# Turning a kernel's token weights on TensorE in float32, with the cast in the eviction, under a new order of all steps

## The chip, the cores and the metric

The kernel runs on one core of a Trainium2 chip. The metric is the device time of one execution in microseconds (us). The engines are TensorE (PE in the profile; its weight loads are listed as PEld), VectorE (DVE), ScalarE (ACT), GpSimd (POOL) and SyncE (SP), which here issues every DMA. TensorE writes to PSUM, eight banks of 128 partitions by 512 float32; VectorE and ScalarE read PSUM, GpSimd doesn't.

## The reference

q, k and v have 8 batches, 8 heads, 576 tokens and 64 columns. Attention has two parts that are added: one over means of four tokens, repeated four times, and one over the neighbours at a distance under 4. The result x, 8 x 576 x 512, goes through a channel-mixing block with token weights:

```
q_d, k_d, v_d = means of 4 tokens;  out_up = repeat(softmax(q_d k_d') v_d, 4)
out_local     = softmax(q k' where |i - j| < 4) v
x             = out_up + out_local, as batch x token x (head, column)
theta = x @ w_theta
zr, zi = x * cos(theta), x * sin(theta)
y = w_tok_r @ zr + w_tok_i @ zi            # 576 x 576 weights over tokens
u = x + y
out = u + max(u @ w_ch, 0)
```

## The kernel before, in words

Each batch runs through the same steps; each has a two-letter name in the code. k and q are loaded (lk, lq) into 16 float32 staging slots (st), cast to bf16 (ck, cq, L296; on VectorE a cast is two instructions, one of 512 columns and one of 64), turned on TensorE (tp, L303) and copied out of PSUM to kT and qT (ev, L316). Means of four tokens are taken on VectorE or GpSimd (kd, qd, L322 or L330 and L333/L336). v is loaded in two halves (lv, lw) and cast (cv, L396); for batch 0 it is loaded in long rows (l1), cast (c1, L372), turned and placed by TensorE (t1, e1, x1, L377 to L394). Scores and their exponentials go through PSUM (sd, ed, ps, ex), the neighbour mask is multiplied in on VectorE or GpSimd (mk, L501), products and normalisation follow (po, nm, nd, xn), and xt and xa give x transposed (xT, L541). Then come theta (th, L552), cosine and sine on ScalarE (cs), z (xm, zz), the mixing with the token weights (mx, L632: eight groups a batch, each of nine matmuls of 288 columns), u (ua, L637), its transposed copy for the residual (up and uc, or the DMA transpose du), the channel weights (ch, L662), the last sum (rl, L667) and the store (st).

The token weights are needed as WT, nine tiles of 128 x 576 bf16 with the summed token on the partitions. The two matrices together have nine row blocks: 0 to 3 are real, 5 to 8 imaginary, and block 4 has the last 64 rows of each. Before, a block is loaded (lb), cast to bf16 into the tiles uT, which serve as room for it (cb, L261), and when all nine are there, each of the nine column tiles is turned by five bf16 transposes into one bank (wp, L273; the last tile by ten) and copied to WT (wc, L278).

The order of the work is written out by hand in ORDER, a list of words: the step's name and a place, which is a staging slot, one or two PSUM banks, or the engine (v VectorE, a ScalarE, g GpSimd). Each engine, and the DMA queue on SyncE, gets its instructions in the order of the list and keeps to it, so a step that waits holds all that stands behind it on its engine. Words that begin with wm are matmuls on zeros (L755) that fill TensorE's time; ts and te load ScalarE's tables (L761). pin() makes the order binding.

Of the kernel before, what the change touches and what calls it, by code (L numbers as in the profile page):

```python
# [41 lines left out]
WPJ = (0, 2, 4, 6, 1, 3, 5, 7, 8)  # L42
# [20 lines left out]
cbg lw cbg cqg lw xa xm1 nm th6 xt23 lv6 evv th7 ts cs xa zz tp45 cbg cbg wp0 cs wcv lv3 xm6 cs tt2 xm3 th7 wp1 lw xm0
zz zz lw qdv lk8 wcv eva ct lk4 lq9 cs cbg cbg cbg cbg wp6 wca wp3 wp2 wp4 wp5 wca wp1 wcv wcv wcv wp2 ztg ps67 ps45
qdg wcv te ex wcv ex lq7 kdg lkb lka zz lkc lqe lkd zp1 zcv cvv lqf mx3 cvg cvg cvg mkv ua cvg lq1 mx2 sd01 ps67 lv0
mkv lq2 ex po45 mx3 nm sd67 ua cqg po45 ed lw po01 nm ua nm mx2 ed ua pv67 po45 lq5 mx3 cqg vda nm nd01 ua cka up2
nd67 mkg cka xn ckg ckg lk6 uca xn up3 tp45 uca tp01 xd6 eva ckg xt23 mx7 xcv eva qdg xa xt45 po01 th6 cqg xa lv3 ckg
lv9 tp23 nm ts cs cqa th4 lq7 xm5 xt01 th6 evv cs tp23 xa zz cqa tt4 ua tp01 kdg cs ct cqg evv ztv th5 lw evv lw xm7
zz cs tp23 mx6 xm4 kdg zp5 qdg ua eva zz cvv ps01 cqa ps23 lv8 xm7 kdg zz zcv lk4 te ex lw mx6 mx4 ua mx5 sd01 mkv lvb
lw ua ex po67 mkv cva ps23 qdg lca lcc utg ed lce nm mx4 cvg ex lcd lvf ua lk1 po01 lk2 sd67 lw po23 ckg nm cqa nm mx5  # L70
ckg ed tp01 cvg ua lq5 eva tp67 mx4 lq0 cca ua up5 evv cvg ua ccg ccg pv23 mkg ucv vda lk3 qdv ps01 ps67 ex up4 mx5
ccv nd23 ex ua nd01 uca kdg ch5 po67 xn ps23 ckg cka lv9 mx4 xn tp01 lw ex mkg rl nm lk6 cva ckg xd5 sd23 ua cqg xcv
xt67 lv7 eva mx4 lw lv4 lw cvg xa lv8 lw ed xt01 po23 po67 th5 ua ch4 cqa ts cs xa nm nm th0 po23 lqb xt67 rl up1 cs
nm kdg th5 xm0 xa cs xm4 tp23 xm6 tt7 mkg cvg zz th0 lqc ucv zz st up1 cvg up5 ch4 eva ucv ckg ct ucv ch1 zz po23 cs
sd67 lve lva rl mkv te ed cvg pv45 lqd lk1 ztg cqg ch0 rl rl lk2 ch1 qdg nm lq3 vda tp67 nd45 rl cqa xm0 lqf eva lw zz
xn nd23 zp1 utg lw xn tp67 zca lk5 lq9 kdg mx0 up1 ua po45 lv0 eva ckg lk7 ps23 nm lw po67 nm ckg lv4 uca mx0 tp45 lk6
qdg mx1 ua xd0 ps67 ua lv8 ex eva xca ckg sd23 xt45 xa lw mx1 mkg st cvg ua ed mx0 ex mx1 mkv ua th0 po23 ua xt45 ts
cs xa xt67 mx1 xm0 xa th4 xm5 lqb zz ua tt0 kdg xm1 cvv ckg cvv th6 ch7 cqg cka cqg cs ct nm cs lvc cqg lk1 ztv tp23
eva lw th0 rl zz cs cqg zz tp67 evv cvg xm4 zz st zp5 zca ch1 rl cva tp23 mx0 po67 ua eva ps45 lw nm po23 lv2 te ex
lv5 mx1 pv67 lke cqg st mx0 po45 dt vda nm lk7 mkv st lqd po23 ckg ua ua qdg sd67 ch1 qdg nm nm ht0 cka ed rt lv3 up6  # L80
up7 cvg ucv uca nd45 kdg cqg nd23 mx0 xn lw xn ps67 ss ps45 ex ex xd2 mx3 tp67 xcv up2 cva ua uca tp45 lq6 rl evv up0
cqg lw eva ch1 ua lvf xt67 ps23 ucv sd45 xa cva st ex lw lq9 rl lk4 mx0 sd23 ed xt67 ua ckg xa lva qdg lw mkv kdv xt45
mx1 cvg th0 ua st lvb mx6 ua lw ed mkg tp23 ts cs utg lw mx7 cqg xa ua up6 po01 po45 cvg eva uca pv23 tt7 nm vda lq0
nm th6 xm0 zz nd45 ct cs ch1 lv1 xn cva st tp23 nd67 cva xn up0 th4 xm5 th6 zz sr eva xm7 xm5 ps23 lv8 lvc rl uca cs
po01 ch4 zz lw cs nm zz ztg ch7 te ex dz xd6 ch5 cvg rl lw lqe utg rl mkg po01 ps23 st mx4 lw lkd up7 cqg cka st ex
up2 uca nm ch3 rl xt01 kdg st st cvg xcv cva qdg ckg ua xa mkg uca po45 pv67 mx2 nm mx0 ua lk6 sd45 vda lk2 rl lq7
xt67 cqg ua ps23 xa mx1 lv5 ed po45 ua lq3 nm st mkv cqg dt ex dk9 sd23 xt67 ckg ed mx0 mkg du xa nd45 ch1 ckg ua po23
xn po67 th0 ts cs th4 tt5 nm cs nd23 rl dkf nm ct cqg evg dka xm1 xm0 mx6 zz th1 th7 cs dk1 cs xm4 xm5 zz ztv xn ua zz
mx6 zz mx4 po23 ua dz xt01 po67 xd5 ua xcv eva lw evg mx4 nm st mx5 eva du xa mx2 ht3 qdg ua mx4 xt01 ua kdg nm ua utg
ps67 du rt cvv du st ps23 kdg ua te ex ex mx5 mx4 ps67 lvb lv0 lw lw qdv xa lv8 sd23 cva xt01 ua mkv xa mkg mx5 ex st  # L90
lv4 ua po67 ua ed nm sd01 ed po23 mkg cvg ch4 ch5 mx0 nm tt1 lw lw cvg cvg rl sr po67 rl dxd po23 ua nm po45 nm ts ct
nm th0 pv67 th1 dx vda ch2 ztg nd45 st st nd67 du xn du xn cs cs du th3 cs th0 xd1 xt45 xt67 rl xcv cs xt23 xa utg dxc
ch1 dx zz ch0 ch4 xa ss ch5 dz th6 zz ch7 dt du xa tt2 zz th3 dxe dx zz st cs rl th1 mx6 cs mx3 ct st ua rl ztv rl cs
dx7 dx mx2 th6 ht4 rt zz mx1 ua mx0 cs rl mx3 mx6 zz dz rl zz ua ua zz mx7 mx1 mx2 ua ua mx0 ua mx3 ua mx6 ua ua mx1
st ua du mx0 st mx2 ua ss utv ch3 ua ua ua st ua utv ch2 ch1 ch0 ch7 ch6 du ch4 du du du du st rl sr rl du du rl dt
ch1 st st rl st rl st st rl rl ht0 rl st st rm su rt sr ss st
# [4 lines left out]
def kernel(  # L101
# [91 lines left out]
    def constants():  # L193
# [3 lines left out]
        nc.vector.memset(warm, 0.0)  # L197
# [61 lines left out]
    def cb(i, w):  # L259
        to = uT[0][:, i, :] if i < 5 else uT[1][:, i - 5, :]  # L260
        COPY[w](out=to, in_=at.pop(("wtok", i)))  # L261
# [15 lines left out]
    def wc(j, w):  # L277
        COPY[w](out=WT[:, j, :], in_=at.pop(("wp", j))[:, 0:S])  # L278
# [520 lines left out]
```

## Time and profile before

| what | value |
|---|---|
| median of 3 runs | 237.85 us (236.62 to 238.53) |
| profiled execution: span from its first to its last instruction | 232.1 us |
| the median less that span | 5.75 us |
| instructions | 9462 |
| DMA | 49.41 MB, mean 213 GB/s |

The profile is of one execution; it gives the span alone, and 5.75 us is what the median of the runs has beside it. Rows are read as follows. A group has its line in the kernel, engine and operation, what it writes and what it reads (partitions x elements, type), its count, busy time, the mean time of one in ns, and the idle time of the engine ahead of it with what ended it. A row of a tile's or a line's view has the least, the median and the longest time of one in ns, and the first and the last start in us. A row of the time line has its start and length in us, and the chain of waits in order of time has the same. A row of stages has the length of the stage, the busy time and number of instructions of each engine in it, the granted share of TensorE's clock, the share of the DMA engines' time, and GB/s.

### The profile page before, as it was taken

What the parts mean: (1) busy time and instruction counts of PE and PEld (TensorE: products, weight loads), DVE (VectorE), ACT (ScalarE), POOL (GpSimd) and SP (SyncE); (2) the same over time, 40 slices, a digit from 0 to 9 for tenths busy, and PEclk for the clock granted to TensorE, in tenths of its full rate; (3) what the DMA queues carried; (4) which work ended last, traced back from release to release, by engine and by line L of the source; (5) the groups of instructions that cost most, each with busy time, mean ns of one, the idle gap of its engine ahead of it and who ended that gap; (6) DMA issues with size and microseconds to landing.
All of it is one profiled execution on the core that took longest, in us unless ns stands there. A gap on an engine that the chain in (4) does not pass through costs nothing.

```text
span 232.1 us, 9462 instructions
## 1 busy us (share of the span) xinstructions
PE 220.7 (95%) x3986; PEld 153.2 (66%) x3986; DVE 191.8 (83%) x365; ACT 156.1 (67%) x241; POOL 135.5 (58%) x179
## 2 busy tenths in 40 slices
PE   7998899999998999999999999999999998999991
PEld 2665678777776765776768766676676563767750
DVE  6699999989997988868997997799889967567572
ACT  3359999799877989867976979857766591620000
POOL 7468989869999656897472837767386510000000
PEclk9999999999999999999999999999999999999998
DMA  6999989999999899989606895899957766556676
GB/s 204 382 392 390 298 134 252 365 263 193 264 263 195 224 290 208 203 209 210 174 3 178 226 234 147 293 249 173 153 122 189 144 138 100 154 126 182 138 235 217
DMA packets 76795, 49.41 MB, mean 213 GB/s; under 512 B 61136, under 2 KB 61392, under 8 KB 76752
## 3 DMA queue, kind: packets, MB, share of 16 engines
q1 hardware_dynamic: 76752, 48.81, 84.6%
q8 instruction: 31, 0.51, 1.1%
q14 instruction: 12, 0.10, 0.2%
HBM read 33.98 MB, written 9.44 MB: 187 GB/s over the span
## 4 chain that ended last, share of the span: by engine, by line
PE 72%; DVE 12%; DMA 5%; SPq 3%; issue 3%; ACT 2%; DVEq 0%
PE PS L632 24%; PE PS L662 10%; PE PS L552 9%; PE PS L303 5%; PE PS L755 4%; PE PS L511 3%; DVE xT L541 3%; DMA out_dram<-osb 2%; DVE pm L501 2%; PE PS L591 2%; PE PS L482 2%; DMA st<-xT 2%; SPq L641 2%; PE PS L533 2%; DVE uT L637 2%
## 5 line engine op out<-in xcount | busy, mean ns | idle before, releaser
L632 PE MATMUL PS<-WT,z 128*128 128x288 bf16 x576 | 77.9, 286 | 1.7 <-issue 1.7
L632 PEld LDWEIGHTS <-z 128*128 128x128 bf16 x576 | 53.8, 98 | 17.5 <-issue 2.8
L637 DVE TENSOR_TENSOR uT<-PS,xT 128x288 bf16<-128x288 f32 x64 | 28.1, 450 | 11.4 <-PE PS L632 11.1
L552 PE MATMUL PS<-wth,xT 128*128 128x512 bf16 x128 | 32.3, 380 | 0.7 <-DVE xT L541 0.7
L557 ACT ACTIVATE cs<-PS,pihc 128x512 bf16<-128x512 f32 x32 | 22.3, 696 | 15.1 <-PE PS L552 9.9
L662 PE MATMUL PS<-wch,uT 128*128 128x512 bf16 (+1 forms) x132 | 30.6, 373 | 0.0
L520 DVE TENSOR_TENSOR tmp<-PS,rl 128x512 bf16<-128x512 f32 x40 | 27.7, 692 | 1.4
L541 DVE TENSOR_TENSOR xT<-PS,xdT 128x928 bf16<-128x928 f32 (+1 forms) x24 | 22.7, 952 | 3.4 <-PE PS L533 3.1
L490 ACT ACTIVATE pm<-PS 128x1024 bf16<-128x1024 f32 (+1 forms) x24 | 20.4, 877 | 7.0 <-PE PS L482 2.7
L501 POOL TENSOR_TENSOR pm<-pm,band 128x1024 bf16<-128x1024 bf16 (+1 forms) x13 | 22.2, 1709 | 2.9 <-ACT pm L490 2.9
L667 DVE SCALAR_TENSOR_TENSOR osb<-PS,ur 128x512 f32<-128x512 f32 (+1 forms) x33 | 21.8, 669 | 2.4 <-PE PS L662 1.6
L330 POOL TENSOR_TENSOR two<-kT 128x580 f32<-128x580 bf16 x15 | 17.5, 1163 | 6.1 <-ACT kT L316 5.2
L296 POOL CAST q_tm<-st 128x576 bf16<-128x576 f32 x22 | 14.4, 664 | 10.8 <-DMA st<-in_q_dram 10.8
L662 PEld LDWEIGHTS <-uT 128*128 128x128 bf16 x132 | 12.2, 98 | 12.2 <-issue 0.3
L558 ACT ACTIVATE cs<-PS 128x512 bf16<-128x512 f32 x32 | 19.4, 605 | 0.0
L330 POOL TENSOR_TENSOR two<-qT 128x576 f32<-128x576 bf16 x11 | 12.8, 1167 | 10.5 <-ACT qT L316 7.1
L552 PEld LDWEIGHTS <-xT 128*128 128x128 bf16 x128 | 11.2, 98 | 10.7 <-issue 1.3
L616 DVE TENSOR_TENSOR z<-PS,cs 128x1024 bf16<-128x1024 bf16 x24 | 16.2, 685 | 1.9 <-PE PS L591 0.9
L437 ACT ACTIVATE pd<-PS 128x864 bf16<-128x864 f32 x16 | 14.1, 889 | 5.2 <-PE PS L426 5.2
L761 ACT ACT_TABLE_LOAD x13 | 16.7, 1283 | 0.2
L296 POOL CAST k_tm<-st 128x576 bf16<-128x576 f32 x21 | 14.4, 695 | 1.4 <-DMA st<-in_k_dram 1.4
L396 POOL CAST v_w<-st 128x512 bf16<-128x512 f32 x21 | 13.3, 653 | 1.3 <-DMA st<-in_v_dram 1.2
(119 smaller groups left out, 419.3 us busy)
## 6 DMA issues: line engine op xcount, KB each, us to landing
st<-in_q_dram SPq DMA_DIRECT2D x32, 288.0 KB, 6.3
st<-in_k_dram SPq DMA_DIRECT2D x32, 288.0 KB, 6.0
st<-in_v_dram SPq DMA_DIRECT2D x70, 128.0 KB, 4.7
out_dram<-osb SPq DMA_DIRECT2D x31, 256.0 KB, 2.9
out_dram<-osb SPq DMA_DIRECT2D x10, 128.0 KB, 2.4
st<-in_v_dram SPq DMA_DIRECT2D x4, 288.0 KB, 3.7
st<-in_moe_w_tok_r_dram SPq DMA_DIRECT2D x4, 288.0 KB, 6.2
st<-in_moe_w_tok_i_dram SPq DMA_DIRECT2D x4, 288.0 KB, 7.2
```

The costliest lines, as they stand in the source:

```text
L296: COPY[w](out=to[:, r, :], in_=of[:, r, :])
L330: nc.gpsimd.tensor_tensor(out=t, in0=src[:, :, 0:2], in1=src[:, :, 2:4], op=ALU.add)
L490: nc.scalar.activation(out=pm[(3 * b + u) % NPM][:, :, 0:n].rearrange("p e c j w -> p e (c j w)"), in_=at.pop(("ps", b, u))[:, :, 0:4 * W ...
L501: EW[w].tensor_tensor(out=t, in0=t, in1=m, op=ALU.mult)
L520: nc.vector.tensor_tensor(out=tmp[(NCH * b + c) % NTMP].rearrange("p g (j d) -> p g j d", d=D), in0=ps[:, :, :, 0:D], in1=r.unsqueeze(3).t ...
L541: nc.vector.tensor_tensor(out=xT[b % 2][:, :, lo:lo + cnt].rearrange("p e (m j) -> p e m j", j=4), in0=at.pop(("xt", b, u))[:, :, 0:cnt].r ...
L552: nc.tensor.matmul(out=ps, lhsT=xT[b % 2][:, dc, P * c:P * c + P], rhs=wth[:, dc, :], start=(dc == 0), stop=(dc == 3))
L557: nc.scalar.activation(out=t[:, 0, :], in_=ps, func=AF.Sin, bias=pihc, scale=1.0)
L632: nc.tensor.matmul(out=ps, lhsT=z[b % 2][:, j, P * dc:P * dc + P], rhs=WT[:, j, cols], start=(j == 0), stop=(j == 8))
L637: nc.vector.tensor_tensor(out=uT[b % 2][:, dc, cols], in0=at.pop(("mx", b, i)), in1=xT[b % 2][:, dc, cols], op=ALU.add)
L662: nc.tensor.matmul(out=ps[:, cols], lhsT=uT[b % 2][:, dc, P * c:P * c + P], rhs=wch[:, dc, cols], start=(dc == 0), stop=(dc == 3))
L667: nc.vector.scalar_tensor_tensor(out=o[:, cols], in0=at["ch", b, c][:, cols], scalar=0.0, in1=ur[b % 2][:, c, cols], op0=ALU.max, op1=ALU.add)
```

## The change

The step cb is gone. wp now takes one row block straight from its float32 staging slot: five transposes with a float32 identity (ident32, a new tile that VectorE copies from ident among the constants) into two neighbouring banks. wc evicts with the cast to bf16: one copy for four tiles' columns and one short copy for tile 8, or two short ones for block 4. Blocks are loaded and turned in the order 0, 5, 1, 6, 2, 7, 3, 8, 4, so a block can be turned as soon as it has landed. WT and all later arithmetic are laid out as before.

```diff
-WPJ = (0, 2, 4, 6, 1, 3, 5, 7, 8)
+WTI = (0, 5, 1, 6, 2, 7, 3, 8, 4)
...
+    def wide(w, n):
+        return PS[:, int(w[0]):int(w[0]) + n, :].rearrange("p k e -> p (k e)")
...
+    ident32 = one([P, P], "ident32", FP32)
...
         nc.vector.memset(warm, 0.0)
+        nc.vector.tensor_copy(out=ident32, in_=ident)
...
-    def cb(i, w):
-        to = uT[0][:, i, :] if i < 5 else uT[1][:, i - 5, :]
-        COPY[w](out=to, in_=at.pop(("wtok", i)))
...
-    def wp(j, w):
-        ps = at["wp", j] = bank16(w)
-        for ri in ((j % 2,) if j < 8 else (0, 1)):
-            lo, n = (0, P) if j < 8 else (HALF * ri, HALF)
-            for ct in ((0, 1, 2, 3, 4), (4, 0, 1, 2, 3))[ri]:
-                base = P * ct - (HALF if ct == 4 and ri else 0)
-                nc.tensor.transpose(out=ps[lo:lo + n, base:base + P],
-                                    in_=(uT[ri][:, ct, :] if ct < 4 else uT[0][:, 4, :])[:, P * (j // 2):P * (j // 2) + n],
-                                    identity=ident)
-
-    def wc(j, w):
-        COPY[w](out=WT[:, j, :], in_=at.pop(("wp", j))[:, 0:S])
+    def wp(i, w):
+        ps = at["wp", i] = wide(w, 2)
+        t = at.pop(("wtok", i))
+        for c in range(4):
+            nc.tensor.transpose(out=ps[:, P * c:P * c + P], in_=t[:, P * c:P * c + P], identity=ident32)
+        nc.tensor.transpose(out=ps[:, 512:512 + P], in_=t[:, S - P:S], identity=ident32)
+
+    def wc(i, w):
+        ps = at.pop(("wp", i))
+        if i == 4:
+            COPY[w](out=WT[:, 0:8, 512:S].rearrange("p (c x) t -> p c x t", x=2),
+                    in_=ps[:, 0:512].rearrange("p (c x t) -> p c x t", x=2, t=HALF))
+            tails = [(ri, 512, HALF * ri, HALF) for ri in range(2)]
+        else:
+            COPY[w](out=WT[:, i // 5:8:2, P * (i % 5):P * (i % 5) + P], in_=ps[:, 0:512].rearrange("p (c t) -> p c t", t=P))
+            tails = [(i // 5, P * (i % 5), 0, P)]
+        for ri, to, of, n in tails:
+            COPY[w](out=WT[HALF * ri:HALF * ri + HALF, 8, to:to + n], in_=ps[HALF:P, 512 + of:512 + of + n])
```

The whole of ORDER is replaced. Its beginning, up to the first scores (ps) of batch 0, before and after:

```diff
-l10 l11 l12 c1v c1a c1g k0 l13 kcv wm061 t101 c1g lq4 e1v wm256 t123 lk5 lk6 kca e1v wm483 x12 x13 lk7 ckv lq8 x10 cka
-lq9 x11 tp45 kcg cqa cva cqg x16 cqg lka cvv cvv lqb evv cvv ckg cva lkc kdg cka cqa lqd ckg lke laf wm772 tp23 evv
-wm754 tp67 pv45 tp01 qdv kcg eva vdv la0 kdg lq1 eva cka wm256 ps23 ex ps67 lk2 qdv ps01 mkv wm446 sd45 sd23 ex ed
+l10 c1v l11 l12 l13 c1a c1v wm761 t101 lk4 lk5 kcv lq6 lq7 lq8 kcv e1v lk9 lk1 lqa ckv kca c1a wm727 t123 e1a ckv
+wm752 x12 cvv x13 cva cqg cqg lk0 lb2 x10 cvv lq3 kcv lbb lv5 tp45 eva kdg cqv x13 lk6 cva x12 lb7 lb8 tp01 eva cvv
+lk4 lqc ckv ckv wm722 pv23 vda cqv wm713 tp45 tp01 wp23 lka evv eva ps01 kdv lb1 ex ps45 wp67 wcv qdg qdg lq2 sd01 la9
...
```

A wm word has a bank, the number of matmuls of 512 columns, and a rest in 64 columns; before there are eight such words (43.9 matmuls of 512 columns in all), after five (17.9), all ahead of the first scores or near them. Over the whole list, the steps that change their engine, with their counts before and after:

| step | VectorE | ScalarE | GpSimd |
|---|---|---|---|
| casts of k and q (ck, cq) | 1, 21 | 20, 6 | 43, 37 |
| masks (mk) | 11, 4 | 0, 0 | 13, 20 |
| means of q (qd) | 5, 0 | 0, 0 | 11, 16 |
| k and q out of PSUM (ev) | 9, 9 | 21, 20 | 2, 3 |
| casts of token weights (cb) | 0, 0 | 1, 0 | 8, 0 |
| copies to WT (wc) | 7, 7 | 2, 2 | 0, 0 |
| xdT out of PSUM (xc) | 7, 3 | 1, 5 | 0, 0 |

ScalarE's table loads by ts and te go from 13 to 15. After, many two-bank tiles use banks that aren't neighbours (po34, nd27, ps57), where before they were always 01, 23, 45 or 67.

More of the change, by code (lines that the diff above doesn't have):

```diff
@@ L63 @@
[L63 to L96, printed above, removed]
+l10 c1v l11 l12 l13 c1a c1v wm761 t101 lk4 lk5 kcv lq6 lq7 lq8 kcv e1v lk9 lk1 lqa ckv kca c1a wm727 t123 e1a ckv
@@ new lines @@
+ps14 ps02 qdg kdg ex ua ch3 ucv xa ex mkv pv45 po67 mkg rl vda ts po02 ch1 dz nm nm th3 mx6 mx0 ua xt67 rl ps12 ua
+po45 nm mx0 kdg xa cs te mx4 xt67 du du du ua qdg ua ex mkg du du po12 sd05 xa nm ht3 rt st ss ch6 ch1 st st sd23 ed
+rl rl po06 nm du sr st st ps57 ex ed ts tt4 ct mkg ch1 rl mx0 ua mx1 ua po02 nm po34 nm po56 th7 th1 nd02 nm dx4 xn
+nd34 st cs dx xn utv cs ch5 rl dx5 mx0 ua mx3 xd0 ua xt45 xt12 xt67 xca xa xa xa ch3 du th0 dx th4 du rl ch1 th3 ch6
+ztv zz zz rl th7 dz cs ch1 dxe zz zz mx0 st st dx ua dx4 dx cs cs tt3 ct rl mx4 mx3 uta dt mx6 rl zz mx1 zz ht0 rt ss
@@ L97 @@
+mx2 ua ua ua ua cs zz th0 cs ua ztg dz zz mx3 ua du du du mx1 ua mx0 mx1 ua ua du mx0 mx1 ua ua mx0 ua st du mx1 ua
+mx0 st mx1 ch3 ua ch0 ua du du sr utg st du ch1 ch2 ch6 ch4 ch7 rl st uta ch3 rl st dt ht0 rl rl rl rl st st rl st st
+st rm su rl st rt ss sr k0
 """
@@ L711 @@
     STEPS = dict(
-        k0=(lambda i, w: None, span(1)), kc=(kc, span(4)), la=(la, span(4)), ca=(ca, span(4)), lb=(lb, span(9)), cb=(cb, span(9)), lc=(lc, span(4)), cc=(cc, span(4)),
-        wp=(wp, [(j,) for j in WPJ]), wc=(wc, [(j,) for j in WPJ]),
+        k0=(lambda i, w: None, span(1)), kc=(kc, span(4)), la=(la, span(4)), ca=(ca, span(4)), lb=(lb, [(i,) for i in WTI]), lc=(lc, span(4)), cc=(cc, span(4)),
+        wp=(wp, [(j,) for j in WTI]), wc=(wc, [(j,) for j in WTI]),
         lk=(load(0), span(B, 4)), lq=(load(1), span(B, 4)), ck=(cast(0), span(B, 4)), cq=(cast(1), span(B, 4)),
```

30 lines of the change are left out of this document (28 added, 2 removed).

## The prediction

> **What bounds the kernel now.** I read the page's busy shares first, then the busy time by stage, then the start of the time line, then the tile and line views of the operations that the change adds.
>
> ```profile
> PE 220.7 (95%) x3986; PEld 153.2 (66%) x3986; DVE 191.8 (83%) x365; ACT 156.1 (67%) x241; POOL 135.5 (58%) x179
> ...
> PE 72%; DVE 12%; DMA 5%; SPq 3%; issue 3%; ACT 2%; DVEq 0%
> PE PS L632 24%; PE PS L662 10%; PE PS L552 9%; PE PS L303 5%; PE PS L755 4%; PE PS L511 3%; DVE xT L541 3%; DMA out_dram<-osb 2%; DVE pm L501 2%; PE PS L591 2%; PE PS L482 2%; DMA st<-xT 2%; SPq L641 2%; PE PS L533 2%; DVE uT L637 2%
> ```
>
> TensorE carries 72% of the chain of waits, and 4% of the chain is L755, matmuls on zeros that the order puts in to fill time. So TensorE is the bound, but not all of its busy time is work. The stages show who stands behind it:
>
> ```profile
> core 0: us, PE busy (x) PEld busy (x) DVE busy (x) ACT busy (x) POOL busy (x), PEclk, DMA share, GB/s
> 0.00:10.00 10.00, 8.74 (x45) 3.98 (x46) 6.88 (x28) 3.04 (x6) 5.95 (x24) 1.00 0.81 274
> 10.00:20.00 10.00, 10.00 (x188) 6.30 (x187) 8.97 (x13) 6.65 (x10) 7.21 (x11) 1.00 1.05 394
> 20.00:50.00 30.00, 28.21 (x721) 22.22 (x721) 28.40 (x57) 27.95 (x43) 24.88 (x32) 1.00 0.99 276
> 50.00:83.00 33.00, 31.85 (x699) 23.18 (x688) 30.41 (x53) 28.09 (x45) 30.02 (x36) 1.00 1.06 229
> 83.00:130.00 47.00, 46.45 (x901) 33.39 (x902) 38.69 (x75) 38.12 (x59) 30.13 (x39) 1.00 0.79 183
> 130.00:180.00 50.00, 49.16 (x988) 34.69 (x977) 44.31 (x78) 38.19 (x57) 33.62 (x35) 1.00 0.90 200
> ```
>
> From 20 to 83 us VectorE is busy 58.8 of 63 us: it has 4.2 us to spare, about as little as TensorE. After 83 us it has some 14 us to spare in 97. What a re-sorting of work costs is therefore decided before 83 us, and by VectorE as much as by TensorE. The granted clock is 1.00 in all these stages, so no term below comes from the clock.
>
> **The change part by part. The token weights.** Before, nine blocks are cast (eight on GpSimd, one on ScalarE), turned in bf16 and copied:
>
> ```profile
> L261 POOL CAST uT<-st 128x576 bf16<-128x576 f32 x8 | 5.1, 669 | 0.1
> L273 PE MATMUL PS<-ident,uT x50: 219/219/243, 31.6 to 36.2; 128*128 128x128 bf16 x40, 128*64 128x128 bf16 x10
> L278 DVE COPY WT<-PS x7: 448/449/458, 32.0 to 36.7; 128x576 bf16<-128x576 bf16 x7
> 34.90 2.27 DVE L278 COPY WT<-PS 128x576 bf16<-128x576 bf16 x6
> 37.26 1.14 PE L632 MATMUL PS<-WT,z 128*128 128x288 bf16 x8
> 37.68 0.42 DVE L586 COPY z<-PS 128x512 bf16<-128x512 bf16 x1
> ```
>
> The last copy ends at about 37.2 and the first mixing matmul (L632) starts at 37.26, so this chain is on the path there. But its ninth matmul needs the z copy that ends at 38.10, so taking the whole chain away moves the start of the mixing by at most 0.9 us: z is late next. I count no gain for it. The casts that go free 5.1 us on GpSimd and one operation on ScalarE.
>
> TensorE loses 50 bf16 transposes and gains 45 in float32. The spacing of transposes and of 512-column matmuls is read from the chain in order of time:
>
> ```profile
> 54.03 0.50 PE PS L303 x9
> ...
> 55.50 0.86 PE PS L552 x4
> ```
>
> Nine transposes take 0.50 us, 0.056 each; four 512-column matmuls take 0.86, 0.215 each. No row here has a float32 matmul. I bound one by these two: 0.056 at best, 0.215 at worst (as if it streamed four times the columns). The 50 cost 2.8 us, the 45 cost 2.5 to 9.7. Of the nine blocks five stand in the new order ahead of the first theta matmul, where TensorE waits and is filled anyway; four stand between it and the first mixing, where TensorE is dense. On the path that is 20 x 0.16 = 3.2 us at worst, and -0.3 at best. I take 0: a transposition moves 128 columns, and the row it is nearest to is the other transposition.
>
> The Trainium skill, "TensorE: Matmul & The Clock Gate", section Terms, has a transpose mode that is 4x faster for FP32, while "FP8 and Floating Point Precision", section TensorE Precision Notes, says that true FP32 takes 4 passes. By the first rule the sum stays as it is, by the second the 3.2 us are due; no run here shows which.
>
> The evictions now read float32 and are two per block, three for block 4. The nearest rows are a float32 eviction and short copies:
>
> ```profile
> L394 DVE CAST v_w<-PS x3: 681/682/692, 10.9 to 13.4; 128x512 bf16<-128x512 f32 x3
> L415 DVE CAST vd<-PS 32x256 bf16<-32x256 f32 x2 | 0.8, 412 | 0.0
> L231 DVE COPY pu<-full 64x32 bf16<-64x32 bf16 x2 | 0.4, 207 | 0.0
> ```
>
> So 0.68 plus a tail of 0.2 to 0.4, say 0.95 for 0.45: seven on VectorE cost 3.5 us more. They are paid below, in VectorE's sum.
>
> **Constants.** The new copy to ident32 stands second on VectorE and waits for GpSimd's mask.
>
> ```profile
> 0.93 0.27 DVE L197 MEMSET warm<- 128x256 uint32 x1 [0.93 <-PEq L783]
> 1.08 0.29 POOL L195 TENSOR_SCALAR_AFFINE_SELECT ident<-ident 128x128 bf16<-128x128 bf16 x1
> 4.54 0.27 DVE L211 COPY vd<-vd 128x16 bf16<-128x16 bf16 x1
> 4.69 0.62 DVE L372 CAST z<-st 128x512 bf16<-128x512 f32 x2
> ```
>
> VectorE would be free at 1.20, the mask is there at 1.37, the copy takes about 0.27: all that is queued behind it, down to the first cast of v, moves by 0.44, and TensorE's first transposes wait for that cast. I take +0.4, between 0 and 0.5.
>
> **Fewer fillers.** Counted from the order, L755 falls from 43.9 to 17.9 matmuls of 512 columns, 26 x 0.215 = 5.6 us of TensorE time before or near the first scores. What was behind them?
>
> ```profile
> 12.78 0.68 ACT L296 CAST k_tm<-st 128x576 bf16<-128x576 f32 x1
> 14.27 1.35 PE L755 MATMUL PS<-warm 128*128 128x512 bf16 x6
> 15.45 0.67 PE L303 MATMUL PS<-ident,k_tm 128*128 128x128 bf16 x9
> 16.16 1.12 ACT L316 COPY kT<-PS 128x1152 bf16<-128x1152 bf16 x1 [2.13 <-PE PS L303]
> ```
>
> The last k tile was cast at 13.46 and the tiles were turned only at 15.45; ScalarE stood idle 2.13 us for it. So the fillers did cost up to 2.0 us here. Elsewhere they cover loads: the DMA share is 0.81 and 1.05 in the first 20 us. The gain lies between 0 and 5.6; I take -1.5, near the 2.0 that the rows show.
>
> **VectorE's new share.** In the new order VectorE takes 21 of the 64 k and q casts, where it had one; 17 stand ahead of batch 1's last mixing group, which starts at 77.7 us before. TensorE's work up to there is 56.3 us in both orders. VectorE's, summed by counts and rows: 16 casts more at 0.62 (+9.9), the WT evictions and ident32 (+3.8), one c1, one cc, one rl, one uc, two kc, one kd more (+4.5); fewer by four q means (-5.4), four k and q evictions (-5.4), two masks (-2.1), one each of ca and vd, two xc, two zc (-3.7). That is +1.6 at the groups' means, of which the large ones are these; nearly even.
>
> ```profile
> L316 DVE COPY kT<-PS 128x1152 bf16<-128x1152 bf16 x6 | 8.1, 1352 | 0.3 <-PE PS L303 0.3
> L322 DVE TENSOR_REDUCE qd<-qT 128x288 bf16<-128x1152 bf16 x5 | 6.7, 1346 | 0.1
> ```
>
> But the price of a cast from SBUF on VectorE isn't fixed:
>
> ```profile
> L396 DVE CAST v_w<-st x5: 410/793/1266, 38.0 to 173.6; 128x512 bf16<-128x512 f32 x5
> L501 DVE TENSOR_TENSOR pm<-pm,band x11: 417/1050/2192, 20.0 to 177.3; 128x1024 bf16<-128x1024 bf16 x9, 128x512 bf16<-128x512 bf16 x2
> 19.97 0.69 DVE L501 TENSOR_TENSOR pm<-pm,band 128x1024 bf16<-128x1024 bf16 x1
> 59.38 1.15 POOL L330 TENSOR_TENSOR two<-kT 128x580 f32<-128x580 bf16 x1
> 59.55 1.27 DVE L396 CAST v_w<-st 128x512 bf16<-128x512 f32 x1
> 176.87 3.69 POOL L501 TENSOR_TENSOR pm<-pm,band 128x1024 bf16<-128x1024 bf16 x2 [1.93 <-ACT pm L490]
> 177.35 2.19 DVE L501 TENSOR_TENSOR pm<-pm,band 128x1024 bf16<-128x1024 bf16 x1
> L296 DVE CAST k_tm<-st x2: 189/308/427, 9.9 to 10.2; 128x512 bf16<-128x512 f32 x1, 128x64 bf16<-128x64 f32 x1
> L396 DVE CAST v_w<-st 128x512 bf16<-128x512 f32 x5 | 4.1, 826 | 0.0
> ```
>
> The same cast takes 0.41 alone and 1.27 when it starts behind a GpSimd operation: it ends 0.29 after the latter. The mask takes 0.69 alone and 2.19 beside GpSimd's. Casts that read PSUM (681 to 692) don't move. The one k cast of before (0.43 + 0.19) ran while GpSimd was idle, so its price is the low end. The five v casts average 0.826, 0.42 over the undisturbed. A k or q cast on VectorE is two instructions, each able to wait: 0.42 to 0.84 more. GpSimd is busy 24.9 of 30 and 30.0 of 33 us in these stages, and its load up to this point stays within 3 us. The first two or three casts run before it has work, so 14 x 0.42 to 0.84 = 5.9 to 11.8; I take the middle, 8.8. With the 1.6 that is 10.4 us on an engine with 4.2 to spare: +6.2 beyond its slack. VectorE and TensorE don't wait at the same moments, and ScalarE gives up casts here, so I put 5.2 on the path, with 0 (the casts wait where nobody waits for them) and 9.2 (13.4 - 4.2) as ends.
>
> The Trainium skill, "SBUF — State Buffer", section Who interferes with whom, says that a VectorE copy or cast in a two-port mode, or an operation with two SBUF inputs, shares a port pair with GpSimd under an exclusive lock, and that the one that issues second waits for the whole instruction. The rows above agree (2.19 for 0.69); by this rule the casts moved here are all of the kind that waits, and it speaks against this change.
>
> **After 83 us.** GpSimd gains masks and q means there, about 17 us in 97, which it has idle (63.75 busy). Two more table loads are ScalarE's, which is idle 20 us of 97. VectorE's count is even within 2 us, with four moved casts. DMA bytes don't change; the loads are in another order, and each queue keeps its count. The tail behind the last mixing has the same nine groups of TensorE. I cost these at nothing; if that cover goes, the masks that move to GpSimd are late next.
>
> **Sum.** Against the profiled execution: span 232.1, and 237.85 with the 5.75 us that the median of the runs lies above it. 237.85 - 1.5 (fillers) + 0.4 (constants) + 0 (float32) + 5.2 (VectorE) = 241.95, about 242.0.
>
> **The rivals.** *Four passes*: the float32 transposes cost four times as much, the case above plus 3.2: 245.2. For it: nothing here has shown a float32 matmul; against it: they are transposes. *Hidden*: VectorE's waits fall where TensorE has other work, 237.85 - 1.5 + 0.4 = 236.75, no change. For it: TensorE's work per stage is the same in both orders. *Start*: the fillers were all on the path, as their 4% of the chain says, and the casts hide too: 237.85 - 5.6 + 0.4 = 232.65, faster. For it: the idle ScalarE at 16.16; against it: the loads of the first 20 us. It decides if the first mixing starts before about 35 us, where it was 37.26.
>
> **How the numbers follow.** VectorE's case has 0.46, four passes 0.10, hidden 0.21, start 0.23. A measurement of this kernel tells about 1% from no change, 235.5 to 240.2. Faster is the start's 0.23, the same the hidden's 0.21, slower the other two, 0.56. The likeliest alone reaches from 236.8 (its 0) to 246 (its 9.2). The range reaches down into the start's case to 234 and up past four passes to 250; some 0.14 lies below and 0.05 above.
>
> **What would show it.** Right: k and q casts on VectorE (L296) with a median well over 0.43 for the large part, and VectorE busy over 30 of 33 us from 50 to 83; batch 1's last mixing later than 77.7. Float32 transposes spaced 0.056 settle the second rival, 0.215 confirm it. Fillers: ScalarE's 2.13 us gone. Wrong: the casts at 0.43 all along, or the first mixing at 35 us with batch 1 ahead of 77.7.

## The result and the profile after

The changed kernel takes 289.3 us (median of 4 runs, 286.84 to 291.03) against 238.2 us (236.62 to 239.24): a ratio of 1.216, 95% interval 1.207 to 1.225. It is 51.1 us slower; the prediction had 242.0, and 250 at the upper end. Ratios and times in brackets, here and below, leave out disturbed runs, those over 1.5% above the fastest of their kernel, so e7 loses one run of 372.9 us, and e3 keeps one of four, 261.0 us, while its ratio alone is of the other three, 265.7 to 268.8 us. The kernel before spreads from 233 to 243 us, so a ratio can differ from the quotient of the medians that stand beside it.

The page of the changed kernel: busy time, TensorE and its granted clock in 40 slices, and the chain of waits by engine.

```profile
PE 231.2 (81%) x3954; PEld 160.0 (56%) x3954; DVE 203.4 (71%) x402; ACT 152.2 (53%) x239; POOL 151.2 (53%) x176
...
PE   7867698689789898876479958687689889999990
...
PEclk9999999999899999999869997799999979999997
...
PE 43%; DVE 21%; ACT 10%; DMA 10%; POOL 8%; issue 6%; SPq 1%; DVEq 0%; ACTq 0%; POOLq 0%
```

TensorE was 95% busy and carried 72% of the chain; now 81% and 43%. VectorE, whose load was to be the price, is busy 11.6 us longer (203.4 for 191.8), but its share of the longer span fell from 83% to 71%. No engine is full: they wait for each other. TensorE's idle time (span less busy) went from 232.1 - 220.7 = 11.4 to 285.1 - 231.2 = 53.9 us, and its busy time went up by 10.5 us for fewer matmuls. The stages, in the columns of the prediction's table:

```profile
20.00:50.00 30.00, 23.57 (x495) 17.91 (x495) 25.32 (x46) 22.89 (x36) 23.12 (x27) 1.00 0.93 248
50.00:83.00 33.00, 26.16 (x511) 19.86 (x510) 28.89 (x52) 20.11 (x31) 23.39 (x27) 0.95 1.08 250
83.00:130.00 47.00, 41.75 (x901) 30.36 (x899) 35.49 (x73) 34.64 (x55) 35.90 (x41) 1.00 0.81 187
130.00:180.00 50.00, 37.12 (x644) 25.28 (x644) 31.63 (x59) 24.21 (x39) 29.36 (x32) 0.90 0.54 135
180.00:230.00 50.00, 39.74 (x742) 26.74 (x742) 33.86 (x65) 26.21 (x43) 25.57 (x21) 0.96 0.37 81
```

TensorE stands idle 6 to 7 us in each of the two early stages (1.8 and 1.2 before), and 13 and 10 us between 130 and 230, where the prediction had put nothing. The clock falls to 0.90 in the stage with the longest waits.

One wait in that stage, on TensorE and then on VectorE (start, length, line, and in brackets the idle time ahead with what ended it):

```profile
167.66 0.40 PE L457 MATMUL PS<-vd,pd 128*72 128x130 bf16 x4
171.80 0.61 PE L596 MATMUL PS<-ident,xT 128*128 128x128 bf16 x4 [3.73 <-DVE xdn L463]
```

```profile
170.82 0.19 DVE L462 RECIPROCAL rd<-PS 72x8 f32<-72x8 f32 x1
171.05 0.69 DVE L463 TENSOR_TENSOR xdn<-PS,rd 72x512 bf16<-72x512 f32 x1
```

TensorE stands idle for 3.73 us before four transposes of x (xm5) and goes on when VectorE has normalised nd46 (xn). The two have no data in common. Their places in the list tell why: nd46 lies on banks 4 and 6, xm5 is to write bank 5. A second one, on ScalarE, VectorE and TensorE:

```profile
179.96 1.94 ACT L495 ACTIVATE pm<-PS 128x1024 bf16<-128x1024 f32 x2 [10.97 <-DVE tmp L525]
```

```profile
178.91 0.21 DVE L524 RECIPROCAL rl<-PS 128x8 f32<-128x8 f32 x1 [0.93 <-PE PS L637]
179.16 0.69 DVE L525 TENSOR_TENSOR tmp<-PS,rl 128x512 bf16<-128x512 f32 x1
```

```profile
176.82 0.46 PE L487 MATMUL PS<-qT,kT 64*64 64x64 bf16 x32
177.10 0.31 PE L516 MATMUL PS<-v_w,pm 64*64 64x65 bf16 x16
...
177.60 1.28 PE L637 MATMUL PS<-WT,z 128*128 128x288 bf16 x9
181.04 0.65 PE L637 MATMUL PS<-WT,z 128*128 128x288 bf16 x4 [2.16 <-ACT pm L495]
```

Read from the bottom: the product po26 (banks 2 and 6) is done at 177.41, but its reciprocal starts when the mixing matmuls on bank 4, between them, end. The scores ps07 (banks 0 and 7, line 487) are done at 177.28, but their exponential waits for the normalisation of po26, on banks between, until 179.96; so 2.7 of ScalarE's 10.97 us are due to it. The next mixing matmuls, on bank 0, need that exponential done and wait 2.16 us.

In the new list 31 two-bank tiles (ps, po, sd, nd) lie on banks that aren't neighbours, from po27 at about 51 us on; in the old list none does. Count each wait in the trace that ended over 0.3 us after the last work on the banks and the data that the waiting instruction does use: the changed kernel has 32 of them, 44.6 us in sum, and the kernel before none. No view of the profile shows this count; a coarser one can be read from the views of waits: TensorE's waits that end with a normalisation on VectorE (tmp or xdn) sum to some 21 us in the changed kernel and 1 us in the kernel before.

**Theory A**: an instruction that reads two banks apart is ordered as if it touched the banks between as well. Rivals: **B**, the order of the steps (VectorE's casts, late loads); **C**, the new way with the token weights itself.

### The profile page after: what moved, and what is told of

It reads as the page before. It is cut to its first block, busy times and chain, and to the rows that moved or that the text cites. A ratio compares the mean times of both kernels' runs of the same rounds, so it can differ in the third digit from the quotient of the medians.

```text
span 285.1 us, 9405 instructions
## 1 busy us (share of the span) xinstructions
PE 231.2 (81%) x3954; PEld 160.0 (56%) x3954; DVE 203.4 (71%) x402; ACT 152.2 (53%) x239; POOL 151.2 (53%) x176
## 4 chain that ended last, share of the span: by engine, by line
PE 43%; DVE 21%; ACT 10%; DMA 10%; POOL 8%; issue 6%; SPq 1%; DVEq 0%; ACTq 0%; POOLq 0%
PE PS L637 19%; PE PS L557 6%; PE PS L667 6%; DMA st<-in_v_dram 4%; DVE tmp L525 3%; DVE k_tm L301 3%; POOL two L335 3%; DMA st<-in_k_dram 2%; DVE xdn L463 2%; DVE osb L672 2%; PE PS L308 2%; ACT pm L495 2%; ACT cs L562 2%; PE PS L516 2%; ACT cs L563 1%
## 5 line engine op out<-in xcount | busy, mean ns | idle before, releaser
L637 PE MATMUL PS<-WT,z 128*128 128x288 bf16 x576 | 82.0, 296 | 11.8 <-ACT pm L495 3.8
L637 PEld LDWEIGHTS <-z 128*128 128x128 bf16 x576 | 56.6, 101 | 30.5 <-issue 13.9
L506 POOL TENSOR_TENSOR pm<-pm,band 128x1024 bf16<-128x1024 bf16 (+1 forms) x20 | 35.8, 1790 | 23.9 <-ACT pm L495 23.9
L642 DVE TENSOR_TENSOR uT<-PS,xT 128x288 bf16<-128x288 f32 x64 | 28.3, 452 | 23.8 <-PE PS L637 19.3
L667 PE MATMUL PS<-wch,uT 128*128 128x512 bf16 (+1 forms) x132 | 33.2, 390 | 3.7 <-DVE osb L672 2.0
L335 POOL TENSOR_TENSOR two<-kT 128x580 f32<-128x580 bf16 x15 | 17.6, 1175 | 11.4 <-ACT kT L321 9.3
L335 POOL TENSOR_TENSOR two<-qT 128x576 f32<-128x576 bf16 x16 | 18.8, 1177 | 8.1 <-DVE qT L321 3.9
L442 ACT ACTIVATE pd<-PS 128x864 bf16<-128x864 f32 x16 | 14.0, 889 | 16.1 <-PE PS L431 12.8
L557 PEld LDWEIGHTS <-xT 128*128 128x128 bf16 x128 | 11.6, 97 | 17.8 <-issue 7.3
L578 POOL TENSOR_TENSOR zT<-xT,cst 128x512 bf16<-128x512 bf16 x5 | 5.8, 1154 | 27.9 <-ACT cst L575 27.9
L321 ACT COPY kT<-PS 128x1152 bf16<-128x1152 bf16 x12 | 13.4, 1119 | 9.2 <-PE PS L308 8.3
```

The costliest lines, as they stand in the source:

```text
L335: nc.gpsimd.tensor_tensor(out=t, in0=src[:, :, 0:2], in1=src[:, :, 2:4], op=ALU.add)
L506: EW[w].tensor_tensor(out=t, in0=t, in1=m, op=ALU.mult)
L557: nc.tensor.matmul(out=ps, lhsT=xT[b % 2][:, dc, P * c:P * c + P], rhs=wth[:, dc, :], start=(dc == 0), stop=(dc == 3))
L637: nc.tensor.matmul(out=ps, lhsT=z[b % 2][:, j, P * dc:P * dc + P], rhs=WT[:, j, cols], start=(j == 0), stop=(j == 8))
L642: nc.vector.tensor_tensor(out=uT[b % 2][:, dc, cols], in0=at.pop(("mx", b, i)), in1=xT[b % 2][:, dc, cols], op=ALU.add)
L667: nc.tensor.matmul(out=ps[:, cols], lhsT=uT[b % 2][:, dc, P * c:P * c + P], rhs=wch[:, dc, cols], start=(dc == 0), stop=(dc == 3))
```

## The experiments

Times are medians, with the time in brackets where it differs; each is beside the kernel before on the same chip.

| run | us | before | ratio, 95% interval |
|---|---|---|---|
| e1 old order, new token weights | 240.0 | 238.6 (235.2) | 1.023, 1.014 to 1.032 |
| e2 before, 31 tiles on banks apart | 268.6 | 238.6 (235.2) | 1.144, 1.133 to 1.154 |
| e3 changed, banks together | 266.0 (261.0) | 238.6 (235.2) | 1.137, 1.119 to 1.155 |
| e4 e3 and loads by need | 258.1 | 236.4 | 1.093, 1.084 to 1.102 |
| e5 e3 and casts on ScalarE | 263.3 (260.6) | 236.4 | 1.102, 1.089 to 1.115 |
| e6 old order, turns spread | 246.8 | 236.4 | 1.043, 1.034 to 1.051 |
| e7 e4 and the old engines | 272.2 | 237.9 (237.2) | 1.149, 1.138 to 1.160 |
| e8 e4 and casts on ScalarE | 253.2 | 237.9 (237.2) | 1.070, 1.061 to 1.078 |
| e9 e1, evictions shared evenly | 239.4 | 237.9 (237.2) | 1.011, 0.998 to 1.023 |
| e10 e8 with the old token weights | 256.8 | 237.7 | 1.074, 1.067 to 1.082 |
| e11 before, loads by need | 235.0 | 237.7 | 0.986, 0.980 to 0.992 |
| e12 old head, new tail | 263.2 (263.0) | 237.6 (236.8) | 1.106, 1.094 to 1.117 |
| e13 new head, old tail | 256.8 | 237.6 (236.8) | 1.082, 1.073 to 1.092 |
| e14 e9, loads by need | 238.3 | 237.6 (236.8) | 1.007, 1.003 to 1.011 |
| e15 changed, readers cut per bank | 261.9 | 237.0 (236.5) | 1.116, 1.095 to 1.137 |
| e16 e8 with the banks apart | 280.2 (279.6) | 237.0 (236.5) | 1.189, 1.164 to 1.214 |

**e1, the new token weights in the old order.** The cast words go; wp and wc as in the change, banks for wp given out anew.

```diff
-cbg cbg cbg cbg wp6 wca wp3 wp2 wp4 wp5 wca wp1 wcv wcv wcv wp2 ztg
+wp23 wp67 wca wp45 wcv wp12 wca wp67 wcv wp34 wcv wp12 wcv wcv ztg
```

> The order of before with the new token weights alone: float32 transposes in two neighbouring banks, the cast in the eviction, ident32, block order 0,5,1,6,...; the cast words go, the nine turns stand about where they stood, each followed soon by its eviction; the fillers stay as in before. No two-bank tile lies on banks that are apart. Theory A (banks): the 31 two-bank tiles of the changed kernel that lie on banks with others between them make engines wait for work on the banks between; without them the time is that of before, 234 to 243 us. Theory B (order): the order of the steps lost the time through VectorE's casts, late loads and SyncE's queue; this order is that of before, so also 234 to 243 us. Theory C (mechanism): the float32 transposes or the strided evictions cost tens of us: 270 us or more.

Measured: 240.0 us. Theory C falls: the token weights cost 1.4 us by the medians, 5.4 by the ratio.

**e2 and e3, bank numbers alone.** In e2 50 words of the old list, in e3 89 words of the new one.

```diff
-ps01
+ps07
...
-ps23
+ps26
...
-po67
+po37
...
```

```diff
-po56 po27
+po67 po12
...
-nd34
+nd45
...
-nd27
+nd23
...
```

> The kernel before with 50 words changed in their bank numbers alone: 31 of its two-bank tiles are put on banks that are not neighbours, from the same place of the list on as in the changed kernel, every bank free for as many words before its reuse as it was. Steps, engines and order are those of before. Theory A (banks): the time goes up by about as much as the changed kernel lost to it, 20 to 50 us, so 258 to 288 us, with waits of ScalarE and TensorE for VectorE's normalisation on other banks. Theory B (order) and theory C (mechanism): 236 to 240 us, no change.

> The changed kernel with 89 words changed in their bank numbers alone, so that all its two-bank tiles lie on neighbouring banks, every bank free for as many words before its reuse as it was. Steps, engines and order are those of the changed kernel. Theory A (banks): of the some 50 us, 32 waits of 44.6 us in sum ended with work on a bank that the waiting instruction doesn't touch; without them 242 to 255 us. Theory B (order) and theory C (mechanism): 284 to 292 us, no change.

Measured: 268.6 us, 30 more for 50 bank numbers (33 by the time in brackets), and 266.0 us, 23 less for 89 (28). The waits defined above: 34 in e2, 49.7 us in sum; none in e3. By the coarser count, TensorE's waits that end with a normalisation sum to some 14 us in e2 and 4 in e3. In e3 the xm that stood 3.73 us:

```profile
159.78 0.40 PE L456 MATMUL PS<-vd,pd 128*72 128x130 bf16 x4
160.02 0.38 PE L595 MATMUL PS<-ident,xT 128*128 128x128 bf16 x4
```

It follows at once. Theory A holds and accounts for about half of the 51 us. e3 is still 26 to 27 us above the kernel before, so theory B has a share too: e3 came out above theory A's 255. Not all of the 44.6 us came back: under such a wait lay others.

**e15, the reader's span.** Were these banks as such at fault? e15 has the changed kernel's list untouched, banks apart included, and cuts the reading instructions.

```diff
-        nc.vector.reciprocal(out=r, in_=ps[:, :, :, 64])
+        for e in cut["po", b, c]:
+            nc.vector.reciprocal(out=r[:, e], in_=ps[:, e, :, 64])
...
```

> The changed kernel as it is, banks apart included (289.3 us); but each step that reads a two-bank tile lying on banks apart reads it with two instructions, one for each bank: 28 exponentials and normalisations become two of half the width. Theory A (the span from the first bank to the last counts as touched by a reading instruction, so it waits for, and holds up, work on the banks between): the wait goes without any change of bank, 264 to 272 us, a little above the kernel with its banks together (266.0) for the added instructions. Rival (these banks themselves are a bad choice, for their reuse or for the access): 286 to 294 us.

Measured: 261.9 us, with 51 instructions more on ScalarE and VectorE (11 exponentials and 20 normalisations were cut, 31 and not 28). At the same place:

```profile
159.27 0.40 PE L465 MATMUL PS<-vd,pd 128*72 128x130 bf16 x4
159.51 0.38 PE L612 MATMUL PS<-ident,xT 128*128 128x128 bf16 x4
```

No bank was moved, and the wait is gone; TensorE's waits that end with a normalisation sum to some 2 us. It is the span of the reading instruction: the program waits by what it takes the instruction to touch, and not for a bank.

**e4, loads in order of need.** In e3's trace, 24 to 95 us (waits: engine, line, what for; us in total, times, longest):

```profile
POOL q_tm L300 <- DMA st<-in_q_dram: 4.1, 1, 4.1
...
DVE v_w L400 <- DMA st<-in_v_dram: 2.9, 1, 2.9
...
DVE k_tm L300 <- DMA st<-in_k_dram: 2.3, 1, 2.3
...
POOL k_tm L300 <- DMA st<-in_q_dram: 1.6, 1, 1.6
```

In the same stretch the kernel before waits once, 0.7 us. The new list has loads for later batches ahead of such that are due.

```diff
-l13
+lk3
...
-lk0 lb2
+lbc lbd
...
-lbb lv5
+lkf lb0
...
```

> The changed kernel with its bank pairs together (266.0 us) and its loads in order of need: the places of the load words in the list stay, but 110 of them hold another load, sorted by the place of the step that uses it (cast or turn), and the staging slots are given out anew, oldest first. Steps on all other engines are untouched. Theory B1 (late loads): in the trace of the kernel with its banks together, batch 1's last half of v is issued at 42.9 us behind five loads for batch 2, and k of batch 3 at 68.8 us behind loads for batch 4; casts waited for such loads some 11 us directly between 24 and 95 us. With the loads by need 250 to 258 us. Theory B2 (VectorE's casts of k and q, the prediction's term): 263 to 268 us, no change. Theory B3 (evictions of the token weights on the path to the first mixing): no change either.

Measured: 258.1 us, 8.0 less by the medians, but only 3.0 by the time in brackets (3.4 by the profiled spans, 259.3 and 255.9). The waits above are gone. So B1 holds, just short of its range, but its size lies open between 3 and 8 us.

**e5 and e8, VectorE's casts.** All ckv become cka, all cqv become cqa; e5 on e3, e8 on e4. What VectorE and TensorE of e4 show:

```profile
66.36 2.54 DVE L300 CAST q_tm<-st 128x512 bf16<-128x512 f32 x4
68.82 0.68 DVE L671 SCALAR_TENSOR_TENSOR osb<-PS,ur 128x512 f32<-128x512 f32 x1
69.42 3.87 DVE L300 CAST k_tm<-st 128x512 bf16<-128x512 f32 x4
```

```profile
69.55 1.02 PE L666 MATMUL PS<-wch,uT 128*128 128x512 bf16 x4 [1.53 <-DVE osb L671]
...
75.00 1.26 PE L636 MATMUL PS<-WT,z 128*128 128x288 bf16 x9 [2.91 <-DVE osb L671]
```

The last sum (osb) that gives a bank free stands in VectorE's queue among the casts, and TensorE waits for the bank.

> The changed kernel with its bank pairs together (266.0 us), and all 21 casts of k and q that VectorE does moved to ScalarE at their places in the list. Theory B2 (VectorE's casts, held up by GpSimd's work, lie on the path; the prediction's term of 5.2 us): 258 to 262 us. Theory B1 (late loads) and B3: 264 to 270 us, no change or a little more, since ScalarE gets some 14 us of work and the loads come as late as before.

> The changed kernel with banks together and loads by need (258.1 us), and the 21 casts of k and q moved from VectorE to ScalarE. With the loads late this move was worth some 3 us (266.0 to 263.3). Theory D1, in the prediction's form (VectorE's casts lie on the path, 5.2 us): 251 to 255 us; in the trace with the loads by need, TensorE waited 1.5 and 2.9 us at 69.6 and 75.0 us behind eight such casts. Theory D2: 257 to 261 us.

Measured: 263.3 us, 2.8 less (0.5 by the times in brackets), while the loads are late, which decides nothing beside e3's spread, and 253.2 us, 4.8 less, once they aren't (e8's runs 252.6 to 253.7, e4's 257.1 to 259.9). That is close to the prediction's own term, 5.2 us, with the banks and the loads put right; what the casts cost in the changed kernel as it stands was not measured alone.

**e16, the three causes in another order.** The list of e8 with the bank numbers of the change.

> The changed kernel with its loads by need and the casts of k and q on ScalarE, but its banks as they are, apart (the kernel with banks together and both of these: 253.2 us; the 89 words between the two are bank numbers alone). If the three causes add up, 289.3 less 8.0 and 4.8: 274 to 279 us. If what the loads and casts cost was only the room that the bank waits left, or the other way round: under 268 or over 285 us.

Measured: 280.2 us, a little above the sum. Banks cost 26.9 us here (e16 less e8; 26.4 in brackets), 23.3 to 28.3 on the change (e3, e15): they add up nearly. Loads and casts together cost 9.1 us with the banks apart (9.7 in brackets) and 12.8 (7.8) with the banks together, so whether the bank waits hide a part of them stays open.

**e7, the old engines.** 127 words of e4 with the engine that did the step before:

```diff
-kcv
+kca
...
-ckv
+cka
...
```

> The changed kernel with banks together and loads by need (258.1 us), and 127 words with another engine: each cast, mask, mean, copy and eviction goes to the engine that did it in the kernel before; the places in the list stay. Theory D1 (the sharing out of the work): after banks and loads the rest of the loss comes from VectorE, which got masks and evictions but above all 21 casts of k and q: 243 to 250 us. Theory D2 (the places of the steps themselves, with the token weights' own cost): 255 to 262 us, no gain.

Measured: 272.2 us, 14 more than e4 and outside both ranges. Theory D1 falls in its general form: as a whole, the new order's sharing out of the work suits the new order better than the old one does. Of its parts only the k and q casts were tried alone (e5, e8).

**e6, e9 and e14, the token weights in the old order.** In e1 the evictions stand in a row on VectorE:

```profile
36.84 0.68 DVE L279 CAST WT<-PS 128x512 bf16<-128x512 f32 x1
37.55 0.29 DVE L282 CAST WT<-PS 64x128 bf16<-64x128 f32 x1
...
43.30 0.47 DVE L282 CAST WT<-PS 64x64 bf16<-64x64 f32 x2
43.78 0.69 DVE L620 TENSOR_TENSOR z<-PS,cs 128x1024 bf16<-128x1024 bf16 x1
```

The last z of batch 0 starts behind them at 43.78, and the first mixing at 43.5 instead of 37.3 us. e6 puts turns and evictions among batch 0's steps, e9 shares e1's row evenly, e14 sorts e9's loads as well.

```diff
-lw xa xm1 nm th6 xt23 lv6 evv th7 ts cs xa zz tp45 cbg cbg wp0 cs wcv
+lw xa xm1 nm wp23 wca th6 xt23 lv6 evv th7 wp45 wcv ts cs xa zz wp23 wcv tp45 wp23 wcv cs
...
```

> The order of before with the new token weights, but turned and evicted one by one among the steps of batch 0 and not bunched after them: first turn after batch 0's first transposes for mixing, the last before its last sine. Evictions of 0.98 us each, six on VectorE and three on ScalarE. Theory B3 (in the earlier run the seven evictions in a row on VectorE, 36.8 to 43.8 us, put the first mixing off from 37.3 to 43.5 us and cost its 5.5 us): 235 to 238 us, first mixing at 38 to 41 us. Rival (the cost is that of the evictions wherever they stand): 239 to 241 us, first mixing at 43 us or later.

> The order of before with the new token weights bunched after batch 0's steps (240.0 us), and the evictions of that bunch shared between ScalarE and VectorE in turn instead of two and five. Theory B3 (the row of evictions on VectorE, 36.8 to 43.8 us, puts off the first mixing by some 6 us): first mixing at 40 to 41.5 us instead of 43.5, and 236.5 to 238.5 us. Rival (the turns or the loads set the first mixing): 239 to 241 us.

> The new token weights at their best here: the order of before, even evictions, and the loads in order of need, which made the kernel before 1.4% faster (235.0 us against 237.7). If the token weights' own cost is what the earlier run showed (1.5 us), 235.5 to 238 us. If earlier loads of the token weights let the new turns start sooner, 232 to 235 us.

Measured: e6 246.8 us, first mixing at 48.1. From 28 to 48 us its turns hold TensorE up, 1.5 us for evictions of token weights ahead of them and 3.3 us for steps of batch 0 (xT, cst), and batch 0's own steps stand behind; the cost is beyond the rival's too. e9: 239.4, first mixing at 41.6, so the time is the rival's, and the mixing comes nearly where B3 put it. e14: 238.3, just above its first range; against e11, the old token weights with the same sorting, that is 3 us (5 by the ratios). At their better places (e1, e9, e14) the new token weights cost 1 to 5 us in this order; evictions of 0.98 us that used to take 0.45 are on the path to the first mixing (in e9 the last ends at about 41.5 and the mixing starts at 41.6).

**e10, the old token weights in the new order.** e8 with casts to bf16 where the turns stood, then bf16 turns.

```diff
-zz wp67 wcv cvg
+zz wp5 wp6 wcv wp4 wca wcv wp7 wcv wp5 wcv wcv cvg
...
```

> The changed kernel with banks together, loads by need and the casts on ScalarE (253.2 us), but with the token weights of before: each block's cast to bf16 stands where its turn stood (eight on GpSimd, one on ScalarE), the bf16 turns and their evictions of 0.45 us follow near the place of the last blocks, seven evictions on VectorE and two on ScalarE. Theory B3 (the float32 evictions of 0.98 us on VectorE put off the first mixing, 42.7 us there against 37.3 us before): first mixing at 38 to 41 us and 247 to 251 us. Theory D2 (the places of the other steps): 252 to 256 us.

Measured: 256.8 us, 3.6 more than e8 (1.2 by the ratios; the chips differ) and outside both ranges. As I placed them the first mixing began only at 47.2 us (42.7 in e8), so it shows no gain to be had there, but not the two ways at equal places.

**e11, the kernel before with its loads by need.** 93 load places hold another load.

```diff
-lq4
+lk4
...
-lq9
+lk9
...
-lqd
+lkd
...
```

> The kernel before with its own loads in order of need: 93 of its load places hold another load, sorted by the place of the step that uses it, staging slots given out anew; all else as it was. If the order of the loads alone is worth time in itself, as it was in the changed kernel (8 us), 230 to 236 us. Rival: the loads of before already come in time, so that its casts don't wait for them, 236 to 240 us.

Measured: 235.0 us, faster by 1.4% (interval 0.8 to 2.0%). This version is ahead of both kernels.

**e12 and e13, two lists put together.** Where are e8's last 14 us over e9? In e12 the words of e9 up to 62 us of TensorE's work come first, then evictions that are due, then those words of e8 that haven't stood yet; e13 has them the other way round.

```diff
-xa cs xm4 tp23 xm6 tt7 mkg cvg zz th0 lqc ucv zz st up1 cvg
+xa cs xm7 tp34 xm5 uca zz evv zz zz lq7 lqc st cqa cqa lve lw
...
```

> A list put together of two: up to some 62 us of TensorE work (about 86 us) the order of before with the new token weights and even evictions (239.4 us in full), from there the changed order with banks together, loads by need and casts on ScalarE (253.2 us in full); PSUM banks and staging slots are given out anew, pairs together. Theory D2a (the rest of the loss lies step by step along the list; at this point the changed order stood 7.5 us behind the other in equal work, and 12.1 us at the end): 242 to 246 us. Theory D2b (it comes from the head alone, what follows only inherits it): 238 to 241 us. Theory D2c (from the tail alone): 250 to 254 us.

> The reverse: the head up to some 62 us of TensorE work from the changed order with loads by need and casts on ScalarE, the tail from the order of before with the new token weights; banks and slots given out anew, pairs together. Theory D2a: 239.4 us and the 7.5 us of the head, 245 to 249 us. Theory D2b: 250 to 254 us. Theory D2c: 238 to 242 us.

Measured: 263.2 and 256.8 us. Both are slower than either parent (239.4 and 253.2), so none of D2a to D2c is told apart. The seam and the newly given banks and slots may cost more than what was looked for; that was not tried. What remains of e8, 15 us over the kernel before, 1 to 5 of it likely the token weights, is not settled.

## Why the prediction was wrong

The direction was right, the size wrong by twelve times: 4.2 us against 51.1. The step that failed is the sum itself: it has no term for the places of the words. It compared the two orders by kind, count and engine of their steps, and said of all after 83 us "I cost these at nothing". The places, the bank numbers above all, were in view but were read as names only. They hold the largest term, 23 to 28 us (e3, e15, e16). It comes from 31 pairs of banks and ran on to the end: from 130 to 230 us TensorE stood idle 23 of 100 us. Some 15 us more, what e8 still has over the kernel before, lie in the order too or in the token weights, and their cause stays open. That the change came out slower, as forecast, is in good part luck: the forecast rested on VectorE's term, a tenth of the loss.

- *VectorE's share, 5.2 us on the path*: near, 4.8 with banks and loads put right (e8), and the mechanism is right too. The casts of the change by form:

```profile
L301 DVE CAST q_tm<-st 128x512 bf16<-128x512 f32 x13 | 7.9, 608 | 0.0
L301 DVE CAST q_tm<-st 128x64 bf16<-128x64 f32 x13 | 5.9, 454 | 0.0
L301 DVE CAST k_tm<-st 128x64 bf16<-128x64 f32 x8 | 5.6, 706 | 0.0
...
L301 DVE CAST k_tm<-st 128x512 bf16<-128x512 f32 x8 | 4.8, 596 | 0.0
```

  24.2 us for 21 casts; undisturbed, at 0.43 + 0.19 each, they would be 13.0. So 0.53 us more for each cast, within the 0.42 to 0.84 that was set, as the exclusive lock in the Trainium skill, "SBUF — State Buffer", section Who interferes with whom, would have it. In the trace each of the 18 cast instructions that took over 0.45 us ends just behind a GpSimd operation that it overlapped, 0.28 to 0.29 us behind it for 512 columns and 0.05 for 64. But "VectorE busy over 30 of 33 us" from 50 to 83 came out as 28.89: the casts hurt by what stood behind them (osb), not by filling the engine. Batch 1's last mixing starts at 92.5 us, later than 77.7, as the prediction's sign asked; but in e8, with these casts on ScalarE, it still starts at 88.9, so the sign doesn't tell the casts from the rest.
- *The loads "are in another order", at no cost*: 3 us by the time in brackets, 8 by the medians (e4).
- *Float32 transposes at 0.056, at worst 0.215*: neither.

```profile
39.43 0.60 PE L270 MATMUL PS<-ident,st 128*128 128x128 f32 x4
39.86 0.27 PE L271 MATMUL PS<-ident,st 128*128 128x128 f32 x1
```

  Four in 0.43 us, 0.11 each: twice the bf16 spacing. The 45 take 4.9 us where the 50 took 2.8. By the prediction's own count, 20 of them on the path, that is 1.0 us where the sum has 0. The rival of four passes falls. Of the two rules of the Trainium skill that the prediction weighed, the transpose mode ("TensorE: Matmul & The Clock Gate", section Terms) and the four passes ("FP8 and Floating Point Precision", section TensorE Precision Notes), the trace agrees with neither in full: 0.11 lies between 0.056 and 0.215, the bounds that the prediction took from its rows.
- *Evictions of 0.95 for 0.45*: right (0.68 + 0.29). They were left within VectorE's sum, but they also stand ahead of the first mixing.
- *Fillers, -1.5, and the rival of the start*: the rival falls. The first mixing begins at 43.8 us, not 35:

```profile
L637 PE MATMUL PS<-WT,z x576: 282/286/448, 43.8 to 270.4; 128*128 128x288 bf16 x192
```

  Nor is ScalarE's wait of 2.13 us gone, the sign that the prediction named for the fillers:

```profile
17.32 1.12 ACT L321 COPY qT<-PS 128x1152 bf16<-128x1152 bf16 x1 [2.11 <-PE PS L308]
```

  What the fillers alone gave was not measured, nor the constants' 0.4.
- *The clock, no term*: the granted clock was 1.00 in all the stages that the prediction looked at; over the changed kernel's execution it was 0.957. How much of TensorE's 10.5 us of added busy time is due to it was not measured apart.
- *The 5.75 us between span and median*: in each of the 17 kernels whose profiled execution has a time, its span lies 1.7 to 1.8 us under that time. So the 5.75 us are not what a run has beside its span: the profiled execution of before took about 233.8 us and was one of the faster ones. The forecast isn't moved by this, for the sum starts from the median, 237.85, and the median beside the changed kernel is 238.2.

## What to carry to other kernels

When an order of work changes, compare the places and not only the counts: a PSUM tile read by one instruction across banks apart is tied to all work on the banks between, and 50 bank numbers alone cost 30 us or more here. Give such tiles neighbouring banks, or read each bank with its own instruction. Sort the loads of a queue by the step that uses them before looking for anything finer; it took 3 to 8 us off the changed kernel and 1.4% off one that looked full.

## What the runs showed of the hardware

- TensorE's granted clock falls after some long waits: behind the stops of 3.42 and 2.13 us in e4 and e3 that are shown below, nine mixing matmuls take 2.34 us at a clock of 0.50, and behind a stop of 1.65 us at the same place in e8 they take 1.28 at 1.00. Over the whole execution the clock was 0.997 in the kernel before, 0.957 in the changed one and 0.978 with the banks together (e3). Of the 25.8 us between the spans of the last two, 18.8 are idle time of TensorE (53.9 and 35.1) and 7.0 its busy time (231.2 and 224.2). But the sum of the idle time doesn't settle the clock: e16 stands idle 51.6 us, and has 0.982 and 224.1 us of busy time.
- A float32 transpose of 128 x 128 through TensorE takes 0.11 us in a row, a bf16 one 0.056.
- In four kernels with the same instructions on TensorE up to there, it stops inside one step (po) with nothing in the trace that ended the wait ("issue"): 1.65 us in e8, and in e4, e3 and e5:

```profile
113.74 0.25 PE L515 MATMUL PS<-v_w,pm 64*64 64x65 bf16 x6 [3.42 <-issue]
...
113.99 2.34 PE L636 MATMUL PS<-WT,z 128*128 128x288 bf16 x9
```

```profile
118.19 0.43 PE L515 MATMUL PS<-v_w,pm 64*64 64x65 bf16 x14 [2.13 <-issue]
```

```profile
120.80 0.42 PE L515 MATMUL PS<-v_w,pm 64*64 64x65 bf16 x13 [3.37 <-issue]
```

  In e4 a transfer of the instruction queue begins within half a microsecond of the stop, among eleven loads. That TensorE waited there for its own instructions behind the loads is a guess that wasn't tried.
